# Flat PSUM quarters, a column-by-column start and an inverse term added last, in a one-core spectral and gated-MLP kernel

## The chip, the cores and the metric

The kernel runs on one core of a Trainium2 chip. The metric is the device time of one execution in microseconds. The engines are TensorE (PE for matmuls, PEld for its weight loads), VectorE (DVE), ScalarE (ACT), GpSimd (POOL) and SyncE (SP, which here only issues DMAs).

## The reference

```
xn  = layernorm(x)                      # x: 2048 x 512, bf16, over the last axis, eps 1e-5
A   = irfft2(rfft2(xn) * (w_r + i w_i)) # over both axes, w: 2048 x 257
B   = (gelu(xn @ w_gate) * (xn @ w_up)) @ w_down   # 512 -> 1792 -> 512
out = x + A + B
```

## The kernel before

The 2048 rows lie as 16 columns c of 128 rows each (row 16 p + c on partition p). Four columns form a block of 512 rows; there are four blocks. Everything is one list of operations with an engine, an expected duration, dependencies and a priority (the smaller, the earlier). A planner (`_Plan.run`) plays this list through once on the host, engine by engine, always taking the ready operation with the smallest priority, and the operations are then emitted in the order it found. So each engine's instruction order is fixed when the program is built; on the chip an engine waits at an instruction until its inputs are there.

The stages:

- **Normalization** (`layernorm`): per column, statistics on DVE (L421), their aggregate on DVE (L428), adding epsilon on POOL (L429), the power −0.5 on POOL (L431), and the scaling to `xn` on DVE (L434). Columns 0 and 1 go singly, 2 and 3 as a pair, the others in fours.
- **Transposes.** Columns 0 to 3 are transposed by PE into PSUM (L444) and copied to `xnT` by DVE (L447); columns 4 to 15 by DMA transposes from SP's queue (L451). Ahead of them PE runs nine dummy matmuls (L409), which need nothing but a memset.
- **Gate and up** (`glu`, L496): for each of 14 slices fc of 128 hidden features, four matmuls into `g_ps` and four into `u_ps`, for 128, 256 or 512 rows at once; gelu on ACT (L505), product on DVE (L510) into `hT`. In block 0 the first two fc are done for column 0, column 1 and the pair (2, 3) separately, the other twelve for all four columns.
- **Forward transform**: folds of `xn` on DVE (L538 to L550), matmuls `bp` (L564) evicted by ACT, then 16 steps `dp` (L600): four matmuls of 128 columns into one PSUM tile, each writing every second word of one half; ACT evicts the tile in order (L605). Then `ep` (L619), the filter on DVE, an exchange of partitions by DMA, and `gp` (L737), whose four matmuls write the four quarters of the tile one after the other.
- **Inverse transform and down** : `yp` (L785) per column with ACT eviction (L791) and unfolding on DVE (L807 to L813), then `down`: 14 matmuls over the hidden features (L837) and one for the inverse transform along the rows (L839), all into one PSUM tile, added to x on DVE (L842) and stored (L845). These fifteen matmuls are one operation of the plan, so it waits for `ID_[c]`, the unfolded inverse of its column.

The last column's down sum is done in two halves. PSUM tiles of the kind "S" (transposes, dummies, both transforms, down sums) share four slots, used in rotation; `g_ps` and `u_ps` have two each. Gate and up units, the spectral steps and the down sums share PE by their priorities, so the spectral chain is strewn among the gate and up matmuls. The loads at the start are issued from SP, the second x column, the identity and the first up weights from ACT. At most eight such transfers are under way at once.

Of the kernel before, what the change touches and what calls it, by code (L numbers as in the profile page):

```python
# [10 lines left out]
P = 128  # L11
BF16 = mybir.dt.bfloat16
F32 = mybir.dt.float32
I32 = mybir.dt.int32
ALU = mybir.AluOpType
# [3 lines left out]
D = 512  # L19
# [4 lines left out]
NFC = DF // P  # L24
NSB = 4
EPS = 1e-5
# [92 lines left out]

class _Buf:  # L120
    def __init__(self, tag):
        self.tag, self.left, self.users = tag, 0, 0


class _Op:
# [3 lines left out]
class _Plan:  # L129
# [17 lines left out]
        return o  # L147

    def run(self):
        free = dict(self.bufs)  # L150
        for o in self.ops:
            for b in o.use:
                b.left = b.users
        waiting = {}
        for o in self.ops:
            waiting.setdefault(o.eng, []).append(o)
        t_eng = {e: 0.0 for e in waiting}
        t_eng["PE"] = t_eng["DVE"] = t_eng["ACT"] = t_eng["POOL"] = t_eng["SP"] = 0.7
        releases, lanes, wire = [], [], 0.0
        order, left, now = [], len(self.ops), 0.0  # L160
        while left:
            releases.sort(key=lambda r: r[0])
            while releases and releases[0][0] <= now + 1e-9:
                free[releases.pop(0)[1]] += 1
            nxt, moved = None, False
            for e, ops in waiting.items():
                if not ops:
                    continue
                if t_eng[e] > now + 1e-9:
                    nxt = t_eng[e] if nxt is None else min(nxt, t_eng[e])  # L170
                    continue
                best = None
                for o in ops:
                    if any(d.end is None for d in o.deps):
                        continue
                    at = max([d.end + d.lag + self.HOP for d in o.deps if d.eng != "PE" or o.eng != "PE"] + [0.0])
                    if o.nbytes and len(lanes) >= 8:
                        at = max(at, sorted(lanes)[-8])
                    if at > now + 1e-9:
                        nxt = at if nxt is None else min(nxt, at)  # L180
                        continue
                    need = {}
                    for b in o.new:
                        need[b.tag] = need.get(b.tag, 0) + 1
                    if any(free[k] < v for k, v in need.items()):
                        continue
                    if best is None or (o.prio, o.n) < (best.prio, best.n):
                        best = o
                if best is None:
                    continue  # L190
                o, moved = best, True
                o.start = now
                o.end = now + o.dur
                t_eng[e] = o.end
                if o.nbytes:
                    wire = max(wire, o.end + 1.0) + o.nbytes / 0.3e6
                    o.end = wire + 0.8
                    lanes.append(o.end)
                    lanes = [x for x in lanes if x > now]
                for b in o.new:  # L200
                    free[b.tag] -= 1
                for b in o.use:
                    b.left -= 1
                    if not b.left:
                        releases.append((o.end + o.lag + self.HOP, b.tag))
                ops.remove(o)
                order.append(o)
                left -= 1
            if not moved:
                if releases:  # L210
                    nxt = releases[0][0] if nxt is None else min(nxt, releases[0][0])
# [9 lines left out]
def kernel(  # L221
# [43 lines left out]
    rstd = pc.tile([P, NC], F32, name="rstd")  # L265
    half = pc.tile([P, NC], F32, name="half")
    warm = pc.tile([P, D], BF16, name="warm")
    tiles = {}

    def cc(name):  # L270
# [39 lines left out]
        return dma(nbytes, fn, deps, n_dma[0] - 1000.0, eng=eng, **k)  # L310

    XD, WD = {}, {}

    def load_x(c0, n, eng="SP"):
        q = nc.sync if eng == "SP" else nc.scalar
        o = load(n * P * D * 2, lambda: q.dma_start(out=x_t[:, c0:c0 + n], in_=x_v[:, c0:c0 + n]), eng=eng)
        for c in range(c0, c0 + n):
            XD[c] = o
# [14 lines left out]
        return load(P * 2 * (b - a), lambda: q.dma_start(out=CT[:, a:b], in_=cap[:, a:b]), eng=eng)  # L333

    load_x(0, 1)
    load_x(1, 1, "ACT")
    d_ident = load_ct("ident", "ident", "ACT")
    load_w(0, 2, ("SP", "ACT"))
    load_x(2, 2)
    load_w(2, 4)  # L340
    load_x(4, 4)
    load_w(4, 7)
# [58 lines left out]
    o_mem = [add("POOL", 0.3, lambda: nc.gpsimd.memset(warm[:], 1.0), (), -20, lag=0.05),  # L401
             add("POOL", 0.2, lambda: nc.gpsimd.memset(half[:], -0.5), (), -15, lag=0.05)]
    wb = _Buf("S")
    NWARM = 9

    def warm_mm(i):
        if i == 0:
            psum("warm", [P, D])
        nc.tensor.matmul(tiles["warm"][:], lhsT=warm[:, 0:P], rhs=warm[:], start=True, stop=True)  # L409

    for i in range(NWARM):
        pe(0.43, lambda i=i: warm_mm(i), (o_mem[0],), -100 + i, new=(wb,) if i == 0 else (), use=(wb,))

# [6 lines left out]
        tiles["st", c] = st  # L420
        V.bn_stats(out=st[:], in_=x_t[:, c])  # L421

    def layernorm(c0, n, due):
        k = slice(c0, c0 + n)
        ag = []
        for c in range(c0, c0 + n):
            s = dve(0.6, lambda c=c: stats(c), (XD[c],), due - 3.0 + 0.01 * (c - c0))
            ag.append(dve(0.08, lambda c=c: V.bn_aggr(out=mv[:, c], in_=tiles["st", c][:]), (s,), due - 3.2, ))  # L428
        e = add("POOL", 0.25, lambda: nc.gpsimd.tensor_scalar(  # L429
            out=ve[:, k], in0=mv[:, k, 1], scalar1=1.0, scalar2=EPS, op0=ALU.mult, op1=ALU.add), ag, due - 5, lag=0.1)  # L430
        r = add("POOL", 0.3, lambda: nc.gpsimd.tensor_tensor(  # L431
            out=rstd[:, k], in0=ve[:, k], in1=half[:, k], op=ALU.pow), (e, o_mem[1]), due - 5, lag=0.1)
        for c in range(c0, c0 + n):
            XN[c] = dve(0.34, lambda c=c: V.tensor_scalar(  # L434
                out=xn[:, c], in0=x_t[:, c], scalar1=mv[:, c, 0:1], scalar2=rstd[:, c:c + 1],
                op0=ALU.subtract, op1=ALU.mult), (r,), due - 2.5)

    def pe_transpose(c, due):
        b = _Buf("S")

        def mm():
            tp = psum(f"tp.{c}", [P, NE, P], BF16)
            for e in range(NE):
                nc.tensor.transpose(tp[:, e], xn[:, c, e * P:(e + 1) * P], ident)  # L444

        o = pe(0.24, mm, (XN[c], d_ident), due - 2, new=(b,))
        XT[c] = dve(0.34, lambda: V.tensor_copy(out=xnT[c // 4][:, :, c % 4], in_=tiles[f"tp.{c}"][:]),  # L447
                    (o,), due - 30, use=(b,))

    def dma_transpose(c, due):  # L450
        XT[c] = dma(P * D * 2, lambda: nc.sync.dma_start_transpose(out=xnT[c // 4][:, :, c % 4], in_=xn[:, c]),  # L451
                    (XN[c],), due - 30, lag=1.0)

    for c0, n, due in ((0, 1, -20), (1, 1, -19), (2, 2, -18)):
        layernorm(c0, n, due)
        for c in range(c0, c0 + n):
            pe_transpose(c, due)
    for b, due in ((1, 16), (2, 24), (3, 32)):
        layernorm(4 * b, 4, due)
        for c in range(4 * b, 4 * b + 4):  # L460
# [55 lines left out]
            HT.setdefault(c, []).append(h)  # L516
        return h

    units = [(0, 1, 0), (0, 1, 1), (1, 1, 0), (1, 1, 1), (2, 2, 0), (2, 2, 1)]
    units += [(0, 4, fc) for fc in range(2, NFC)]  # L520
    for u in units:
        glu(*u)

# [70 lines left out]
    def dstep(G, t):  # L594
        sb, db = _Buf("S"), _Buf("ds")

        def mm():
            dp = psum(f"dp.{G}", [P, 2, P, 2])
            for q in range(4):
                nc.tensor.matmul(dp[:, q % 2, :, q // 2], lhsT=Bs[:, q, G].rearrange("p c r a -> p (c r a)"),  # L600
                                 rhs=FQ[q], start=(q == 0), stop=(q == 3), skip_group_check=True)

        def ev():
            ds = work(f"ds.{G}", [P, D], "ds")
            nc.scalar.copy(out=ds[:], in_=tiles[f"dp.{G}"][:].rearrange("p s k t -> p (s k t)"))  # L605

        p = pe(0.34, mm, [PS_[cg, q] for cg in range(4) for q in range(4)] + [d_ct], t, new=(sb,))
        DS_[G] = act(0.53, ev, (p,), t - 5, new=(db,), use=(sb,)), db

    def cstep(g, t):  # L610
# [210 lines left out]
    def down(c, t):  # L821
# [8 lines left out]
        for k in range(parts):  # L830
# [3 lines left out]
            def mm(k=k, s=s):  # L834
                y = psum(f"yp_.{c}.{k}", [P, D])
                for f in range(NFC):
                    nc.tensor.matmul(y[:, s], lhsT=tiles[sb, f][:, cl * P:(cl + 1) * P], rhs=tiles["Wd"][:, f, s],  # L837
                                     start=(f == 0), stop=False)
                nc.tensor.matmul(y[:, s], lhsT=tiles["RI"][:, c], rhs=tiles["yt"][:, c, s], start=False, stop=True)  # L839

            p = pe(15 * 0.2158 / parts, mm, HT[c] + d_wd + [d_ri, ID_[c]], t + k * 0.01, new=(pb,))
            a = dve(0.61 / parts, lambda k=k, s=s: V.tensor_tensor(  # L842
                out=tiles[f"y.{c}"][:, s], in0=tiles[f"yp_.{c}.{k}"][:, s], in1=tiles[f"y.{c}"][:, s], op=ALU.add),
                (p, l), t - 40, use=(pb, yb))
# [43 lines left out]
```

## Time and profile before

| | |
|---|---|
| median of 3 runs | 189.26 us (188.01 to 189.47) |
| the profiled execution | 188.04 us |
| its span | 186.3 us |
| mean granted clock of TensorE | 0.988 |
| busy: PE, DVE, ACT, POOL | 176.2, 119.2, 93.2, 16.7 us |

The span is the time from the first to the last recorded instruction of the profiled execution; 1.74 us lie around it. A row of the order of time gives start, duration, engine, line, operation, output and inputs, the count of instructions merged, and in brackets the idle time before it with what ended it. A row of groups gives count, total busy time, mean duration in ns, idle time before, and what ended that. PE's busy time is that of overlapping records, so a group of matmuls costs the distance to the next group's start, not its own duration. The chain of work that ended last has these distances already. In rows of DMA issues the last number is the time from issue to landing, in us.

### The profile page before, as it was taken

The numbers are of one execution on the slowest core, as the hardware profiler recorded it, in microseconds if no ns is written. First come the engines' busy times: TensorE is split into PE (matmuls) and PEld (weight loads), VectorE is DVE, ScalarE is ACT, GpSimd is POOL, SyncE is SP. The second block draws the span as 40 slices with busy tenths as digits, with TensorE's granted clock in tenths as the row PEclk, the third lists the DMA queues.
The fourth block names the chain that finished last, engine by engine and source line by source line (L and its number), as shares of the span: only waits on it lengthen the run. The fifth ranks groups of instructions, "written<-read, shape, count | busy, mean of one in ns | idle before, by whom it ended". The sixth has DMA issues, their size and how long they took to land.

```text
span 186.3 us, 2911 instructions
## 1 busy us (share of the span) xinstructions
PE 176.2 (95%) x1014; PEld 93.5 (50%) x1032; DVE 119.2 (64%) x264; ACT 93.2 (50%) x169; POOL 16.7 (9%) x35
## 2 busy tenths in 40 slices
PE   7379999999999999999999999998999999999993
PEld 2266445546545545556456545455444444444462
DVE  1779989989248999888586888247712134433521
ACT  2023348898986878798969864457200011121100
POOL 3312176230020000000000000000000000000000
PEclk9879999999999999999999999999999999999999
DMA  5999999933356010222011020200021313122111
GB/s 158 332 351 351 347 193 232 234 76 56 113 177 221 0 42 14 58 56 62 14 42 43 18 56 0 56 4 0 11 75 56 115 58 113 58 83 86 58 58 55
DMA packets 23038, 19.24 MB, mean 103 GB/s; under 512 B 8240, under 2 KB 21680, under 8 KB 23024
## 3 DMA queue, kind: packets, MB, share of 16 engines
q1 hardware_dynamic: 21888, 17.44, 35.4%
q0 software_dynamic: 320, 1.19, 2.3%
q10 hardware_dynamic: 816, 0.43, 0.8%
q8 instruction: 8, 0.13, 0.3%
q14 instruction: 6, 0.05, 0.1%
HBM read 13.28 MB, written 2.10 MB: 83 GB/s over the span
## 4 chain that ended last, share of the span: by engine, by line
PE 90%; DMA 3%; DVE 2%; ACT 2%; issue 1%; SPq 0%; DVEq 0%
PE g_ps L496 26%; PE u_ps L496 26%; PE dp L600 4%; DMA x_t<-in_A_x_dram 3%; PE bp L564 2%; PE gp L737 2%; PE ep L619 2%; PE yp__1693 L837 2%; PE yp__2023 L837 2%; PE yp__1880 L837 2%; PE yp__1849 L837 2%; PE yp__1804 L837 2%; PE yp__1784 L837 2%; PE yp__1744 L837 2%; PE yp__1725 L837 2%; PE yp__2049 L837 2%
## 5 line engine op out<-in xcount | busy, mean ns | idle before, releaser
L496 PE MATMUL g_ps<-xnT,Wg_sb 128*128 128x512 bf16 (+2 forms) x232 | 58.4, 370 | 1.7 <-DVE xnT L447 1.4
L496 PE MATMUL u_ps<-xnT,Wu_sb 128*128 128x512 bf16 (+2 forms) x235 | 58.3, 368 | 0.3
L510 DVE TENSOR_TENSOR hT<-u_ps,ge 128x512 bf16<-128x512 f32 (+2 forms) x60 | 39.0, 651 | 23.5 <-PE u_ps L496 21.7
L505 ACT ACTIVATE ge<-g_ps 128x512 bf16<-128x512 f32 (+2 forms) x60 | 34.2, 570 | 32.0 <-PE g_ps L496 29.2
L496 PEld LDWEIGHTS <-Wg_sb 128*128 128x128 bf16 x240 | 23.7, 103 | 24.4 <-DVE xnT L447 1.2
L837 PEld LDWEIGHTS <-hT 128*128 128x128 bf16 x238 | 23.0, 98 | 23.6 <-issue 0.2
L496 PEld LDWEIGHTS <-Wu_sb 128*128 128x128 bf16 x240 | 23.2, 100 | 23.2
L791 ACT CAST yf<-yp 128x512 bf16<-128x512 f32 x16 | 8.8, 588 | 39.3 <-PE yp L785 38.9
L627 ACT CAST E<-ep 64x512 bf16<-64x512 f32 x32 | 18.5, 579 | 3.9 <-PE ep L619 2.4
L421 DVE BATCH_NORM_STATS2 st<-x_t 128x6 f32<-128x512 bf16 x16 | 10.4, 668 | 5.2 <-DMA x_t<-in_A_x_dram 5.2
L605 ACT CAST ds<-dp 128x512 bf16<-128x512 f32 x16 | 8.6, 592 | 2.6 <-PE dp L600 2.6
L743 ACT CAST Gs<-gp 128x512 bf16<-128x512 f32 x16 | 8.7, 589 | 0.8 <-PE gp L737 0.8
L568 ACT CAST Bs<-bp 128x512 bf16<-128x512 f32 x16 | 8.5, 601 | 0.0
L600 PE MATMUL dp<-CT,Bs 128*128 128x128 bf16 x64 | 8.3, 309 | 0.0
L378 ACT COPY TW<-Ts 128x514 bf16<-128x514 bf16 (+1 forms) x12 | 8.0, 701 | 0.0
L600 PEld LDWEIGHTS <-Bs 128*128 128x128 bf16 x64 | 6.8, 129 | 1.6
L434 DVE TENSOR_SCALAR xn<-x_t,mv,rstd 128x512 bf16<-128x512 bf16 x16 | 5.8, 407 | 1.1 <-POOL rstd L431 1.1
L785 PE MATMUL yp<-CT,Gs 128*128 128x128 bf16 x64 | 5.7, 219 | 0.3
L785 PEld LDWEIGHTS <-Gs 128*128 128x128 bf16 x64 | 4.5, 97 | 3.0 <-issue 0.7
L660 DVE TENSOR_TENSOR m<-X,TW 128x1024 bf16<-128x1024 bf16 x8 | 5.5, 688 | 0.2
L666 DVE TENSOR_TENSOR m<-X,TW 128x1024 bf16<-128x1024 bf16 x8 | 5.5, 682 | 0.0
L737 PEld LDWEIGHTS <-F 128*128 128x128 bf16 x64 | 4.2, 98 | 1.9
(104 smaller groups left out, 169.5 us busy)
## 6 DMA issues: line engine op xcount, KB each, us to landing
y<-in_A_x_dram SPq DMA_DIRECT2D x16, 128.0 KB, 2.1
F<-F SPq DMA_DIRECT2D x32, 64.0 KB, 2.0
out_dram<-y SPq DMA_DIRECT2D x15, 128.0 KB, 1.7
Wd_sb<-in_B_w_down_dram SPq DMA_DIRECT2D x2, 896.0 KB, 7.4
x_t<-in_A_x_dram SPq DMA_DIRECT2D x3, 512.0 KB, 8.5
Wg_sb<-in_B_w_gate_dram SPq DMA_DIRECT2D x2, 384.0 KB, 7.4
Wu_sb<-in_B_w_up_dram SPq DMA_DIRECT2D x2, 384.0 KB, 7.8
Wg_sb<-in_B_w_gate_dram SPq DMA_DIRECT2D x2, 256.0 KB, 5.0
```

The costliest lines, as they stand in the source:

```text
L421: V.bn_stats(out=st[:], in_=x_t[:, c])
L496: nc.tensor.matmul(p[:, 0:w], lhsT=W[:, e, fc * P:(fc + 1) * P], rhs=rhs(e), start=(e == 0), stop=(e == NE - 1))
L505: nc.scalar.activation(out=e[:, 0:w], in_=tiles[f"g_ps.{key}"][:, 0:w], func=AF.Gelu_apprx_tanh)
L510: V.tensor_tensor(out=hslot(sb, fc)[:, o:o + w], in0=tiles[f"u_ps.{key}"][:, 0:w], in1=tiles[f"ge.{key}"][:, 0:w], op=ALU.mult)
L568: nc.scalar.copy(out=o, in_=tiles[f"bp.{cg}.{q}"][:].rearrange("p c (r g a) -> p (c r) g a", r=2, a=4))
L600: nc.tensor.matmul(dp[:, q % 2, :, q // 2], lhsT=Bs[:, q, G].rearrange("p c r a -> p (c r a)"), rhs=FQ[q], start=(q == 0), stop=(q == 3), ...
L605: nc.scalar.copy(out=ds[:], in_=tiles[f"dp.{G}"][:].rearrange("p s k t -> p (s k t)"))
L627: nc.scalar.copy(out=tiles[f"E.{g}"][64 * h:64 * h + 64, r], in_=tiles[f"ep.{g}.{h}"][64 * r:64 * r + 64])
L743: nc.scalar.copy(out=o, in_=tiles[f"gp.{g}.{h}"][:].rearrange("p q (n a) -> p (q n) a", a=4))
L785: nc.tensor.matmul(yp[:, q], lhsT=tiles["G"][:, q, c], rhs=IQ[q], start=(q == 0), stop=(q == 3), skip_group_check=True)
L791: nc.scalar.copy(out=tiles[f"yf.{c // 2}"][:, c % 2], in_=tiles[f"yp.{c}"][:])
L837: nc.tensor.matmul(y[:, s], lhsT=tiles[sb, f][:, cl * P:(cl + 1) * P], rhs=tiles["Wd"][:, f, s], start=(f == 0), stop=False)
```

## The change

- **`dp`**: the tile is declared [2, 2, 128] in place of [2, 128, 2], so that each of the four matmuls writes 128 words in a row. The eviction reads the tile by a permuted view, so `ds` is laid out as before. The expected duration in the plan goes from 0.34 to 0.222.
- **Start**: columns 0 to 3 are normalized one by one; column 1's statistics wait for column 0's aggregate. The addition of epsilon is done by DVE in all groups. The transposes of columns 0 to 3 are copied by ACT. Ten dummies in place of nine, and four more of 128 columns after each of the first two transposes. The x columns 2 and 3 are loaded singly, column 1 from SP's queue. A gelu of one element per partition, on a tile filled by POOL, stands early on ACT. Slices fc 0 to 3 of block 0 are now split: fc 0 and 1 for column 0 and for column 1, fc 2 and 3 for the pair (0, 1), and all four for the pair (2, 3).
- **`down`**: the 14 matmuls and the inverse term are two operations; only the second waits for the unfolded inverse and the row table.
- **Planner**: it follows the rotation of the slots (a tile is given a slot when the tile that held that slot is done) rather than a count of free slots.

```diff
     def run(self):
-        free = dict(self.bufs)
+        rings = {tag: [] for tag in self.bufs}
...
-                    need = {}
-                    for b in o.new:
-                        need[b.tag] = need.get(b.tag, 0) + 1
-                    if any(free[k] < v for k, v in need.items()):
+                    held = [rings[b.tag][-self.bufs[b.tag]] for b in o.new if len(rings[b.tag]) >= self.bufs[b.tag]]
+                    if any(b.free is None for b in held):
+                        continue
+                    at = max([b.free for b in held] + [0.0])
+                    if at > now + 1e-9:
+                        nxt = at if nxt is None else min(nxt, at)
                         continue
...
+    o_eps = add("POOL", 0.15, lambda: nc.gpsimd.memset(eps[:], EPS), (), -30, lag=0.05)
...
     load_x(0, 1)
-    load_x(1, 1, "ACT")
     d_ident = load_ct("ident", "ident", "ACT")
+    load_x(1, 1)
     load_w(0, 2, ("SP", "ACT"))
-    load_x(2, 2)
+    add("ACT", 1.3, lambda: nc.scalar.activation(out=eps[:, 1:2], in_=eps[:, 0:1], func=AF.Gelu_apprx_tanh),
+        (o_eps,), -900)
+    load_x(2, 1)
+    load_x(3, 1)
     load_w(2, 4)
...
-    NWARM = 9
+    NWARM, NGAP, GAP = 10, 2, 4
...
-    def layernorm(c0, n, due):
+    def layernorm(c0, n, due, after=()):
...
-            s = dve(0.6, lambda c=c: stats(c), (XD[c],), due - 3.0 + 0.01 * (c - c0))
+            s = dve(0.6, lambda c=c: stats(c), [XD[c]] + list(after), due - 3.0 + 0.01 * (c - c0))
...
-        e = add("POOL", 0.25, lambda: nc.gpsimd.tensor_scalar(
-            out=ve[:, k], in0=mv[:, k, 1], scalar1=1.0, scalar2=EPS, op0=ALU.mult, op1=ALU.add), ag, due - 5, lag=0.1)
+        e = dve(0.07, lambda: V.tensor_scalar(
+            out=ve[:, k], in0=mv[:, k, 1], scalar1=EPS, scalar2=None, op0=ALU.add), ag, due - 5)
...
-        XT[c] = dve(0.34, lambda: V.tensor_copy(out=xnT[c // 4][:, :, c % 4], in_=tiles[f"tp.{c}"][:]),
+        XT[c] = act(0.45, lambda: nc.scalar.copy(out=xnT[c // 4][:, :, c % 4], in_=tiles[f"tp.{c}"][:]),
...
-    for c0, n, due in ((0, 1, -20), (1, 1, -19), (2, 2, -18)):
-        layernorm(c0, n, due)
-        for c in range(c0, c0 + n):
-            pe_transpose(c, due)
+    first = ()
+    for c, due in ((0, -28), (1, -25), (2, -22), (3, -19)):
+        o = layernorm(c, 1, due, first if c == 1 else ())
+        first = o if c == 0 else first
+        pe_transpose(c, due)
+        if c < NGAP:
+            dummies(GAP, due - 1.9, (XN[c],), P)
...
-    units = [(0, 1, 0), (0, 1, 1), (1, 1, 0), (1, 1, 1), (2, 2, 0), (2, 2, 1)]
-    units += [(0, 4, fc) for fc in range(2, NFC)]
+    units = [(0, 1, 0), (0, 1, 1), (1, 1, 0), (1, 1, 1), (0, 2, 2), (0, 2, 3)]
+    units += [(2, 2, fc) for fc in range(4)] + [(0, 4, fc) for fc in range(4, NFC)]
...
-            dp = psum(f"dp.{G}", [P, 2, P, 2])
+            dp = psum(f"dp.{G}", [P, 2, 2, P])
             for q in range(4):
-                nc.tensor.matmul(dp[:, q % 2, :, q // 2], lhsT=Bs[:, q, G].rearrange("p c r a -> p (c r a)"),
+                nc.tensor.matmul(dp[:, q % 2, q // 2], lhsT=Bs[:, q, G].rearrange("p c r a -> p (c r a)"),
...
-            nc.scalar.copy(out=ds[:], in_=tiles[f"dp.{G}"][:].rearrange("p s k t -> p (s k t)"))
+            nc.scalar.copy(out=ds[:].rearrange("p (s k t) -> p s k t", s=2, t=2),
+                           in_=tiles[f"dp.{G}"][:].rearrange("p s t k -> p s k t"))
...
-                nc.tensor.matmul(y[:, s], lhsT=tiles["RI"][:, c], rhs=tiles["yt"][:, c, s], start=False, stop=True)
-
-            p = pe(15 * 0.2158 / parts, mm, HT[c] + d_wd + [d_ri, ID_[c]], t + k * 0.01, new=(pb,))
+            def mm2(k=k, s=s):
+                nc.tensor.matmul(tiles[f"yp_.{c}.{k}"][:, s], lhsT=tiles["RI"][:, c], rhs=tiles["yt"][:, c, s],
+                                 start=False, stop=True)
+
+            p = pe(14 * 0.2158 / parts, mm, HT[c] + d_wd, t + k * 0.01, new=(pb,))
+            p = pe(0.2158 / parts, mm2, [p, d_ri, ID_[c]], t + k * 0.01 - 2, use=(pb,))
```

More of the change, by code (lines that the diff above doesn't have):

```diff
@@ L121, in __init__ @@
     def __init__(self, tag):
-        self.tag, self.left, self.users = tag, 0, 0
+        self.tag, self.left, self.users, self.free = tag, 0, 0, None
 class _Op:
@@ L158, in run @@
         t_eng["PE"] = t_eng["DVE"] = t_eng["ACT"] = t_eng["POOL"] = t_eng["SP"] = 0.7
-        releases, lanes, wire = [], [], 0.0
+        lanes, wire = [], 0.0
         order, left, now = [], len(self.ops), 0.0
         while left:
-            releases.sort(key=lambda r: r[0])
-            while releases and releases[0][0] <= now + 1e-9:
-                free[releases.pop(0)[1]] += 1
             nxt, moved = None, False
@@ L200, in run @@
                 for b in o.new:
-                    free[b.tag] -= 1
+                    rings[b.tag].append(b)
                 for b in o.use:
@@ L204, in run @@
                     if not b.left:
-                        releases.append((o.end + o.lag + self.HOP, b.tag))
+                        b.free = o.end + o.lag + self.HOP
                 ops.remove(o)
@@ L209, in run @@
             if not moved:
-                if releases:
-                    nxt = releases[0][0] if nxt is None else min(nxt, releases[0][0])
                 if nxt is None or nxt <= now:
@@ L267 @@
     warm = pc.tile([P, D], BF16, name="warm")
+    eps = pc.tile([P, 2], F32, name="eps")
     tiles = {}
@@ L403, with warm_mm, dummies @@
     wb = _Buf("S")
-    NWARM = 9
-    def warm_mm(i):
-        if i == 0:
+    NWARM, NGAP, GAP = 10, 2, 4
+    def warm_mm(w):
+        if "warm" not in tiles:
             psum("warm", [P, D])
-        nc.tensor.matmul(tiles["warm"][:], lhsT=warm[:, 0:P], rhs=warm[:], start=True, stop=True)
-    for i in range(NWARM):
-        pe(0.43, lambda i=i: warm_mm(i), (o_mem[0],), -100 + i, new=(wb,) if i == 0 else (), use=(wb,))
+        nc.tensor.matmul(tiles["warm"][:, 0:w], lhsT=warm[:, 0:P], rhs=warm[:, 0:w], start=True, stop=True)
+    def dummies(n, prio, deps=(), w=D):
+        for i in range(n):
+            pe(w / 1200.0, lambda w=w: warm_mm(w), [o_mem[0]] + list(deps), prio + 0.01 * i,
+               new=() if wb.users else (wb,), use=(wb,))
+    dummies(NWARM, -100)
     XN, XT = {}, {}
@@ L426, in layernorm @@
         for c in range(c0, c0 + n):
-            s = dve(0.6, lambda c=c: stats(c), (XD[c],), due - 3.0 + 0.01 * (c - c0))
-            ag.append(dve(0.08, lambda c=c: V.bn_aggr(out=mv[:, c], in_=tiles["st", c][:]), (s,), due - 3.2, ))
-        e = add("POOL", 0.25, lambda: nc.gpsimd.tensor_scalar(
-            out=ve[:, k], in0=mv[:, k, 1], scalar1=1.0, scalar2=EPS, op0=ALU.mult, op1=ALU.add), ag, due - 5, lag=0.1)
-        r = add("POOL", 0.3, lambda: nc.gpsimd.tensor_tensor(
+            s = dve(0.6, lambda c=c: stats(c), [XD[c]] + list(after), due - 3.0 + 0.01 * (c - c0))
+            ag.append(dve(0.15, lambda c=c: V.bn_aggr(out=mv[:, c], in_=tiles["st", c][:]), (s,), due - 3.2, ))
+        e = dve(0.07, lambda: V.tensor_scalar(
+            out=ve[:, k], in0=mv[:, k, 1], scalar1=EPS, scalar2=None, op0=ALU.add), ag, due - 5)
+        r = add("POOL", 0.55, lambda: nc.gpsimd.tensor_tensor(
             out=rstd[:, k], in0=ve[:, k], in1=half[:, k], op=ALU.pow), (e, o_mem[1]), due - 5, lag=0.1)
         for c in range(c0, c0 + n):
-            XN[c] = dve(0.34, lambda c=c: V.tensor_scalar(
+            XN[c] = dve(0.36, lambda c=c: V.tensor_scalar(
                 out=xn[:, c], in0=x_t[:, c], scalar1=mv[:, c, 0:1], scalar2=rstd[:, c:c + 1],
                 op0=ALU.subtract, op1=ALU.mult), (r,), due - 2.5)
+        return ag
     def pe_transpose(c, due):
@@ L604, in ev @@
             ds = work(f"ds.{G}", [P, D], "ds")
-            nc.scalar.copy(out=ds[:], in_=tiles[f"dp.{G}"][:].rearrange("p s k t -> p (s k t)"))
-        p = pe(0.34, mm, [PS_[cg, q] for cg in range(4) for q in range(4)] + [d_ct], t, new=(sb,))
+            nc.scalar.copy(out=ds[:].rearrange("p (s k t) -> p s k t", s=2, t=2),
+                           in_=tiles[f"dp.{G}"][:].rearrange("p s t k -> p s k t"))
+        p = pe(0.222, mm, [PS_[cg, q] for cg in range(4) for q in range(4)] + [d_ct], t, new=(sb,))
         DS_[G] = act(0.53, ev, (p,), t - 5, new=(db,), use=(sb,)), db
```

## The prediction

> **What bounds the kernel now.** I read the page first, then the span cut into stretches, then the chain of work that ended last, and last the order of time at the two ends of the program.
>
> ```profile
> span 186.3 us, 2911 instructions
> PE 176.2 (95%) x1014; PEld 93.5 (50%) x1032; DVE 119.2 (64%) x264; ACT 93.2 (50%) x169; POOL 16.7 (9%) x35
> ```
> ```profile
> 4.00:14.00 10.00, 5.69 (x54) 4.38 (x52) 7.42 (x23) 1.11 (x4) 2.38 (x6) 0.83 1.07 341
> 14.00:45.30 31.30, 31.09 (x186) 16.39 (x189) 30.09 (x66) 20.59 (x39) 11.61 (x16) 1.00 0.98 221
> 49.40:101.34 51.94, 51.63 (x293) 28.12 (x298) 40.02 (x91) 42.61 (x76) 1.21 (x6) 1.00 0.25 72
> ```
>
> The columns of a stretch are its length and the busy time of PE, PEld, DVE, ACT and POOL, then granted clock, DMA share and GB/s. From 14 us on PE is never without work, so there only fewer or cheaper matmuls, or a PE that reaches this stretch sooner, can help. Before 14 us PE is busy 5.69 of 10 us, at a mean clock of 0.83: that is where time lies open. DVE is busy 30.09 of 31.30 us up to 45.3, ACT 42.61 of 51.94 after 49.4; both are near enough to full to be watched.
>
> The profiled execution took 188.04 us, 1.74 beside its span; the median of the runs shown is 189.26, 1.2 above. The sum is made from 188.04. About 1% (1.9 us) is what a measurement of this kernel can tell from no change.
>
> **The start.** In order of time:
>
> ```profile
> 1.31 3.64 PE L409 MATMUL warm<-warm 128*128 128x512 bf16 x9 [1.31 <-POOL half L402]
> 4.00 0.69 DVE L421 BATCH_NORM_STATS2 st<-x_t 128x6 f32<-128x512 bf16 x1 [4.00 <-DMA x_t<-in_A_x_dram]
> 5.21 0.17 DVE L428 BATCH_NORM_AGGREGATE mv<-st 128x2 f32<-128x6 f32 x1
> 6.01 0.58 POOL L431 TENSOR_TENSOR rstd<-ve,half 128x1 f32<-128x1 f32 x1
> 6.71 0.69 DVE L421 BATCH_NORM_STATS2 st<-x_t 128x6 f32<-128x512 bf16 x1 [1.21 <-DMA x_t<-in_A_x_dram]
> 7.33 0.40 DVE L434 TENSOR_SCALAR xn<-x_t,mv,rstd 128x512 bf16<-128x512 bf16 x1
> 7.78 1.01 PE L444 MATMUL tp<-CT,xn 128*128 128x128 bf16 x8 [2.83 <-DVE xn L434]
> 8.63 0.41 DVE L447 COPY xnT<-tp 128x512 bf16<-128x512 bf16 x1
> 9.09 0.59 PE L496 MATMUL g_ps<-xnT,Wg_sb 128*128 128x128 bf16 x4 [0.30 <-DVE xnT L447]
> 10.32 0.63 PE L496 MATMUL u_ps<-xnT,Wu_sb 128*128 128x128 bf16 x4
> 10.75 0.63 PE L496 MATMUL g_ps<-xnT,Wg_sb 128*128 128x128 bf16 x4
> 11.45 0.39 PE L496 MATMUL g_ps<-xnT,Wg_sb 128*128 128x128 bf16 x4
> 11.67 0.39 PE L496 MATMUL u_ps<-xnT,Wu_sb 128*128 128x128 bf16 x4
> 13.85 0.61 PE L496 MATMUL g_ps<-xnT,Wg_sb 128*128 128x256 bf16 x4 [1.05 <-DVE xnT L447]
> 14.29 0.60 PE L496 MATMUL u_ps<-xnT,Wu_sb 128*128 128x256 bf16 x4
> 19.06 1.03 PE L496 MATMUL g_ps<-xnT,Wg_sb 128*128 128x512 bf16 x4
> ```
>
> Three losses are seen. Column 0 has its statistics by 4.69, but its aggregate stands behind column 1's statistics until 5.21, and its normalization at 7.33 behind column 2's. The transpose at 7.78 is copied only at 8.63, behind DVE's next statistics. And PE was idle 2.83 us, so its clock fell: four narrow matmuls go every 0.43 us (10.32 to 10.75) until about 11.2, and every 0.22 us after (11.45 to 11.67).
>
> After the change column 1's statistics wait for column 0's aggregate, so that goes at 4.69. The addition of epsilon moves to DVE; no row shows it there. Bounds are a small gain (POOL's own addition and a hop go away) and 0.40 us, the wide normalization's row; I take 0.17, as the aggregate's row has no more elements. So 4.69 + 0.17 + 0.17 + 0.58 for the power and two hops of 0.1 between engines (an estimate; 7.73 to 7.78 is 0.05 from DVE to PE): normalization at 5.8, transposes at 6.25 (7.33 to 7.78 now), at full clock done by 6.65. The copy on ScalarE is not in the trace; its nearest rows are DVE's own copy above, 0.41, and an eviction of as many elements:
>
> ```profile
> L791 ACT CAST yf<-yp 128x512 bf16<-128x512 f32 x16 | 8.8, 588 | 39.3 <-PE yp L785 38.9 <-DVE lv L809 0.4
> ```
>
> These are the bounds, with the eviction's 0.59 taken, since it is the same engine reading PSUM; ACT is busy 1.11 us of ten here, so nothing stands behind the copy. So the first gate matmul starts at **7.3** in place of 9.09. DVE sheds four copies and takes seven small additions: nearly even.
>
> The ten dummies end near 5.2 (one more at 0.22 us, and the memset of epsilon ahead of them, some 0.1). PE then idles 1.05 us to 6.25. An idle time of just 1.05 us, at 13.85, did not slow the four matmuls behind it (0.44 us for 256 columns). So I reckon at full clock; the short dummies behind the first two transposes lie under the copies. From 7.3: eight groups of narrow matmuls at 0.22 (1.76), twelve of 256 columns at 0.44 (5.28), two transposes and the last dummies (0.66): fc 4 starts at **15.0** in place of 19.06. The early table load and the wait for epsilon stand in ACT's idle time, with no copy due before 6.65; behind that wait on ACT is nothing but compute.
>
> Column 1 moves from ACT's queue to SP's, ahead of the first gate weights; the split of columns 2 and 3 adds one issue.
>
> ```profile
> 1.65 0.52 ACTq L326 DMA_DIRECT2D Wu_sb<-in_B_w_up_dram  x1
> 2.19 0.43 SPq L326 DMA_DIRECT2D Wg_sb<-in_B_w_gate_dram  x1
> ```
> ```profile
> Wu_sb<-in_B_w_up_dram ACTq DMA_DIRECT2D x1, 256.0 KB, 6.0
> Wg_sb<-in_B_w_gate_dram SPq DMA_DIRECT2D x1, 256.0 KB, 6.1
> SPq L316 <- DMA x_t<-in_A_x_dram: 1.0, 1, 1.0
> ```
>
> The first up weights land at 7.65 now; issued 0.45 us sooner with 128 KB less ahead on their queue they land at 6.5 to 7.2, in time for 7.5. The second gate weights land at 8.3. Their up half becomes the ninth transfer, the one that waits for the first to land (4.0 us); at the 341 GB/s of this stretch its 256 KB come 0.75 us behind, at about 9.1, and PE wants them at 9.7. That is tight by half a microsecond.
>
> **Where the start's gain is cut.** Block 1 needs the DMA transposes of columns 4 to 7:
>
> ```profile
> 24.43 2.60 SPq L451 DMA_TRANSPOSE xnT<-xn  x1
> ```
> ```profile
> xnT<-xn SPq DMA_TRANSPOSE x1, 9.2
> SPq L451 <- DMA Wu_sb<-in_B_w_up_dram: 0.9, 1, 0.9
> ```
> ```profile
> 36.52 0.89 PE bp L564 x16
> 38.27 0.86 PE g_ps L496 x4
> ```
>
> The first of the four was held by the landing of a weight transfer (second row of waits), the fourth, issued at 24.43, landed at 33.63. The same bytes stand ahead of them after the change, so I leave 33.63. PE would come to block 1 at 15.0 + 10 units of 1.73 (twice 0.86) + one transform group of 0.89 = 33.2; it must wait to 33.7. Now it comes there at 38.27 less 0.17 (a group's record of 1.03 at 19.06 against the chain's 0.86: records overlap), 38.1, with one transform group (0.89) more done: 37.2. **Gain 3.5**, not 4.1. The wait absorbs half a microsecond of error in the start.
>
> **The forward transform.**
>
> ```profile
> 63.39 0.87 PE dp L600 x8
> 73.77 0.45 PE gp L737 x8
> ```
> ```profile
> L605 ACT CAST ds<-dp 128x512 bf16<-128x512 f32 x16 | 8.6, 592 | 2.6 <-PE dp L600 2.6
> L600 PEld LDWEIGHTS <-Bs 128*128 128x128 bf16 x64 | 6.8, 129 | 1.6
> ```
>
> Eight dp matmuls take 0.87 us and eight gp of the same shape 0.45; gp writes its quarters flat, dp every second word. Flat, each of the eight pairs saves 0.42: **3.4**. The eviction now reads words from two quarters by turns. No row reads PSUM so; its bounds are 0.59 (nothing changes) and 1.18 (each word dear twice, as for dp). I take 0.59: ScalarE wants one word where PE writes two in the same time (512 columns in 0.216 us against 0.588 for the row). ACT's 42.61 us of work then stand in some 49 us, and small waits of PE on it are likely: I charge **0.5**. DVE finishes the folds only some 2 us sooner, as it is full to 45.3; gate and up matmuls of blocks 1 to 3 cover that, and it would cost 1.5 us without them.
>
> **The end of the gate and up work.**
>
> ```profile
> 126.66 2.93 PE L785 MATMUL yp<-CT,Gs 128*128 128x128 bf16 x32
> 127.08 2.56 ACT L791 CAST yf<-yp 128x512 bf16<-128x512 f32 x5 [0.49 <-PE yp L785]
> 128.49 0.42 DVE L811 TENSOR_TENSOR yt<-lv 128x512 bf16<-128x512 bf16 x1
> 129.69 3.18 PE L837 MATMUL yp__1693<-Wd_sb,hT 128*128 128x512 bf16 x13
> ```
>
> Eight inverse steps take 3.03 us here, paced by ScalarE's evictions, and would take 0.22 each by the gp row, which has the same form: 1.25 us lost. The first down sums no longer wait for their inverse term, so they stand between the steps: **1.2**. The number of matmuls is unchanged, as is the tail behind the last one.
>
> Sum: 188.04 − 3.5 − 3.4 − 1.2 + 0.5 = **180.4 us**, chance 0.68.
>
> **Rivals.**
> - *The DMA transposes come later.* If the added transfer shifts the landing that the first one waits for by one place, to the x columns behind the weights (512 KB at 341 GB/s are 1.5 us), block 1 starts 1.5 later: 181.9. For it: transfers wait on each other eight back. Against: the transposes move one place too. 0.08.
> - *The clock is not held.* If it falls in the 1.05 us, or is granted late, the narrow work runs at half speed for some 1.5 us more; fc 4 comes at 16.5, block 1 at 34.7: 181.4. 0.06. [...]
> - *The eviction costs double.* 16 more times 0.43 us (half of the 0.86 that 512 words at half rate would take) makes ACT's work 6.9 longer: 49 us in 49, so PE waits some 3: 183.4. 0.06.
> - *The change does not do what it says at dp:* its weight loads (129 against 98 ns) set the pace, not the writes. Nothing of the 3.4: 183.8. Against: a load's 129 ns is already more than the spacing of 109 ns (0.87 by 8), so loads overlap and need not set it. 0.05. [...]
> - *Slower: down sums hold the PSUM ring.* A down sum now keeps one of four S slots until its inverse term is there. If three stand ahead of the next inverse pair, that pair waits, and its chain of eviction and unfolding (126.66 to 128.9, 2.25 us) lies open. Over eight pairs that is 18 us: 199. From five pairs on it is slower than now. Against: inverse steps are ordered more than two columns ahead. 0.04.
>
> **How the numbers follow.** The low end: no wait for the transposes (4.1 for the start), the copy and the epsilon at their low ends (0.35), no charge on ACT, the full 1.25 at the end: 178.9, and 0.4 for what executions differ, 178.5. The high end: the fourth rival's 183.8 and the 1.2 us between profile and median, 185.0. What lies outside is the last rival and 0.03 for several losses together that bring it within 1%; all else is faster by over 1%: 0.93, 0.03, 0.04.
>
> **What the changed profile would show.** First gate matmul near 7.3, clock at 1.0 from about 5 us on, fc 4 near 15; PE waiting for DMA at the start of block 1, near 33.7; eight dp in 0.45 us with ds rows still near 590 ns; down sums standing among the first inverse steps, with no waits of PE behind ScalarE there. The prediction is wrong if ds rows are over 0.8 us, if weights land after 7.5 or 9.7, or if PE has gaps over 1 us after 34 us.

## The result, and the profile after

The changed kernel takes **181.22 us** (median of 4 runs, 180.84 to 181.63) against 189.25 before (4 runs, one more than shown above): a ratio of 0.9589, 95% interval 0.9542 to 0.9635. Forecast were 180.4 us in a range of 178.5 to 185.0. The profiled execution took 181.31 us, 1.81 beside its span.

The page, and two stretches of the span (length, then PE, PEld, DVE, ACT and POOL busy, clock, DMA share, GB/s):

```profile
span 179.5 us, 2986 instructions
PE 173.6 (97%) x1057; PEld 91.0 (51%) x1057; DVE 117.9 (66%) x269; ACT 95.6 (53%) x176; POOL 16.4 (9%) x31
```
```profile
4.00:14.00 10.00, 9.33 (x95) 7.22 (x94) 8.80 (x30) 4.68 (x12) 2.21 (x4) 1.00 1.05 341
14.00:45.30 31.30, 30.68 (x185) 15.91 (x184) 28.53 (x66) 20.46 (x39) 11.48 (x13) 1.00 0.88 213
```

Up to 14 us PE is now busy 9.33 of 10 us at a granted clock of 1.00 (5.69 at 0.83 before). From 14 to 45.3 us it is busy a little less than before (30.68 against 31.09): new waits are there. The start in order of time:

```profile
1.34 4.45 PE L411 MATMUL warm<-warm 128*128 128x512 bf16 x10 [1.34 <-POOL half L404]
3.65 0.69 DVE L427 BATCH_NORM_STATS2 st<-x_t 128x6 f32<-128x512 bf16 x1 [3.65 <-DMA x_t<-in_A_x_dram]
5.52 0.41 DVE L440 TENSOR_SCALAR xn<-x_t,mv,rstd 128x512 bf16<-128x512 bf16 x1
5.99 0.61 PE L451 MATMUL tp<-CT,xn 128*128 128x128 bf16 x4 [0.20 <-DVE ve L435]
6.39 0.63 PE L411 MATMUL warm<-warm 128*128 128x128 bf16 x4
6.63 0.58 ACT L454 COPY xnT<-tp 128x512 bf16<-128x512 bf16 x1 [3.45 <-PE tp L451]
7.27 0.38 PE L506 MATMUL g_ps<-xnT,Wg_sb 128*128 128x128 bf16 x4 [0.25 <-ACT xnT L454]
8.38 0.39 PE L506 MATMUL u_ps<-xnT,Wu_sb 128*128 128x128 bf16 x4
9.00 0.38 PE L506 MATMUL g_ps<-xnT,Wg_sb 128*128 128x128 bf16 x4 [0.23 <-ACT xnT L454]
15.57 1.89 PE L506 MATMUL g_ps<-xnT,Wg_sb 128*128 128x512 bf16 x8
32.01 1.03 PE L506 MATMUL g_ps<-xnT,Wg_sb 128*128 128x512 bf16 x4
33.31 1.02 PE L506 MATMUL u_ps<-xnT,Wu_sb 128*128 128x512 bf16 x4 [0.27 <-DVE hT L520]
34.17 1.03 PE L506 MATMUL g_ps<-xnT,Wg_sb 128*128 128x512 bf16 x4
35.77 0.84 PE L574 MATMUL bp<-RF_t,xf 128*128 128x128 bf16 x12 [0.35 <-DVE xf L560]
69.48 1.02 PE L506 MATMUL u_ps<-xnT,Wu_sb 128*128 128x512 bf16 x4 [0.37 <-DVE hT L520]
```

The first gate matmul stands at 7.27, fc 4 at 15.57, block 1 at 34.17. The four transposes at 5.99 take 0.40 us and the ten dummies 4.45, about 0.43 each for 512 columns: that is half the pace of the groups from 7.27 on (0.22), although the granted clock is 1.00 in the row above. The spectral steps and the first down sums, from the chain of work that ended last and from the groups:

```profile
74.39 0.45 PE dp L610 x8
121.41 0.45 PE yp L796 x8
121.86 3.02 PE yp__1688 L848 x14
```
```profile
L615 ACT CAST ds<-dp 128x512 bf16<-128x512 f32 x16 | 9.0, 590 | 1.1 <-PE dp L610 1.0
L610 PEld LDWEIGHTS <-Bs 128*128 128x128 bf16 x64 | 4.3, 98 | 1.9
```

Eight dp matmuls take 0.45 us, their eviction by turns from two quarters 590 ns (592 before), and a down sum begins right behind the third inverse step. Three places remain where PE waits after 16 us (33.31, 35.77 and 69.48). The first is between 32.01 and 33.31: 1.30 us for a group of 0.86. Its cause lies on ScalarE:

```profile
29.02 0.62 ACT L380 COPY TW<-Ts 128x514 bf16<-128x514 bf16 x1 [3.15 <-DMA Ts<-in_A_w_r_dram]
16.66 1.09 POOL L365 DMA_INDIRECT Ts<-in_A_w_r_dram,idx_t  x1 [0.18 <-issue]
30.17 0.69 DVE L520 TENSOR_TENSOR hT<-u_ps,ge 128x512 bf16<-128x512 f32 x1 [2.24 <-ACT ge L515]
```
```profile
Ts<-in_A_w_r_dram SPq DMA_DIRECT2D x2, 224.9 KB, 13.2
```

ScalarE waited 3.15 us for filter rows loaded from SP, with a gelu behind the wait in its queue; a product on DVE waited 2.24 us for that gelu. The chain of work that ended last goes through this load, and from it by the gelu and DVE to PE at 35.77:

```profile
15.80 13.14 DMA Ts<-in_A_w_r_dram
```

Before the change the same two loads landed 10.4 us after issue (these lines give KB of one and the median from issue to landing), the gathers of the other filter rows on GpSimd began at 24.14 us and no copy waited:

```profile
Ts<-in_A_w_r_dram SPq DMA_DIRECT2D x2, 224.9 KB, 10.4
```
```profile
24.14 1.10 POOL L363 DMA_INDIRECT Ts<-in_A_w_r_dram,idx_t  x1 [0.17 <-issue]
27.52 0.62 ACT L378 COPY TW<-Ts 128x514 bf16<-128x514 bf16 x1
```

The gathers moved because the plan gave GpSimd another order. Before, the addition and the power of columns 8 to 11 (at 22.34 and 22.96) stood ahead of them; now that power (23.60) stands behind them.

### The profile page after: what moved, and what is told of

Read it like the earlier page. It is cut to its first block, busy times and chain, and to the rows that moved or that the text cites. A ratio compares the mean times of both kernels' runs of the same rounds, so it can differ in the third digit from the quotient of the medians.

```text
span 179.5 us, 2986 instructions
## 1 busy us (share of the span) xinstructions
PE 173.6 (97%) x1057; PEld 91.0 (51%) x1057; DVE 117.9 (66%) x269; ACT 95.6 (53%) x176; POOL 16.4 (9%) x31
## 4 chain that ended last, share of the span: by engine, by line
PE 73%; DMA 9%; DVE 7%; SPq 6%; issue 2%; ACT 1%; ACTq 0%; DVEq 0%
PE u_ps L506 18%; PE g_ps L506 17%; DMA Ts<-in_A_w_r_dram 7%; SPq L325 3%; DMA Wu_sb<-in_B_w_up_dram 2%; PE yp L796 2%; PE gp L748 2%; SPq L315 2%; DVE hT L520 2%; PE yp__2064 L848 2%; PE yp__2037 L848 2%; PE yp__2006 L848 2%; PE yp__1921 L848 2%; PE yp__1890 L848 2%; PE yp__1863 L848 2%; PE yp__1832 L848 2%
## 5 line engine op out<-in xcount | busy, mean ns | idle before, releaser
L515 ACT ACTIVATE ge<-g_ps 128x512 bf16<-128x512 f32 (+2 forms) x62 | 35.0, 564 | 21.9 <-PE g_ps L506 15.6
L506 PEld LDWEIGHTS <-Wg_sb 128*128 128x128 bf16 x248 | 23.2, 98 | 22.0 <-issue 0.8
L802 ACT CAST yf<-yp 128x512 bf16<-128x512 f32 x16 | 9.3, 586 | 38.1 <-PE yp L796 38.1
L437 POOL TENSOR_TENSOR rstd<-ve,half 128x1 f32<-128x1 f32 (+1 forms) x7 | 6.7, 955 | 24.8 <-DVE ve L435 24.8
L411 PE MATMUL warm<-warm 128*128 128x512 bf16 (+1 forms) x18 | 5.5, 469 | 1.3 <-POOL half L404 1.3
L630 PE MATMUL ep<-ds,CT 128*128 128x512 bf16 x16 | 5.6, 379 | 0.0
```

Source lines behind the costliest of these rows:

```text
L506: nc.tensor.matmul(p[:, 0:w], lhsT=W[:, e, fc * P:(fc + 1) * P], rhs=rhs(e), start=(e == 0), stop=(e == NE - 1))
L515: nc.scalar.activation(out=e[:, 0:w], in_=tiles[f"g_ps.{key}"][:, 0:w], func=AF.Gelu_apprx_tanh)
L802: nc.scalar.copy(out=tiles[f"yf.{c // 2}"][:, c % 2], in_=tiles[f"yp.{c}"][:])
```

## Experiments: the parts one by one

The kernel before, measured again beside each of three groups of runs, had medians of 188.95, 188.89 and 189.56 us, so a difference between kernels of different groups is good to about half a microsecond.

**The flat tile alone**, put into the kernel before:

```diff
-            dp = psum(f"dp.{G}", [P, 2, P, 2])
+            dp = psum(f"dp.{G}", [P, 2, 2, P])
...
-        p = pe(0.34, mm, ...
+        p = pe(0.222, mm, ...
```

> The kernel before with the flat dp tile, its permuted eviction and its shorter planned duration alone. Theory (the writes of every second word set dp's pace): eight dp matmuls in 0.45 us, eviction rows near 590 ns, 3.4 us less than before, ratio near 0.982. Rival (another engine paces the chain there, or the work goes into a new wait): less than 1.5 us.

185.54 us (185.25 to 185.64) against 188.95, ratio 0.9814 (0.9786 to 0.9841): 3.4 us. In its chain and groups:

```profile
63.16 0.45 PE dp L600 x8
```
```profile
L605 ACT CAST ds<-dp 128x512 bf16<-128x512 f32 x16 | 8.7, 592 | 1.8 <-PE dp L600 1.7
```

The term stands at its full size, and nothing of it went into a wait.

**The old tile in the changed kernel** (the same edit backwards):

> The changed kernel with the old dp tile, eviction and planned duration. Theory (terms add up): 3.4 us more than the changed kernel, about 184.6. Rival (the order of the plan or the fuller ScalarE ate part of the gain): 2 us more or less than that, 182 to 183.2.

184.00 us (183.56 to 185.39), 2.8 more than the changed kernel's 181.22; eight dp take 0.87 us again. This lies between the two expectations. The runs of this kernel differ by 1.8 us, so the missing 0.6 is not settled.

**The old start in the changed kernel**: normalization, copies, loads, dummies and units of `before`, with flat dp, split down sums and the new planner.

> The changed kernel with everything of the start as before (normalization of 2 and 3 as a pair, copies on DVE, epsilon on POOL, nine dummies, old loads and units); flat dp, split down sums and new planner stay. Theory (block 1 starts 3.1 us sooner with the new start, and some 1 us of that goes into waits of PE on DVE behind it): 2 to 3.1 us more than the changed kernel, 183.2 to 184.3. Rival (the start is absorbed by the load stream later): under 1 us more.

183.95 us (182.93 to 184.99): 2.7 more, as the theory had it. In its profiled execution narrow matmuls went at half pace for longer than in that of the kernel before:

```profile
9.64 0.58 PE L493 MATMUL g_ps<-xnT,Wg_sb 128*128 128x128 bf16 x4 [0.28 <-DVE xnT L444]
12.58 0.63 PE L493 MATMUL u_ps<-xnT,Wu_sb 128*128 128x128 bf16 x4
13.01 1.06 PE L441 MATMUL tp<-CT,xn 128*128 128x128 bf16 x8
```

Eight narrow groups run from 9.64 to 13.01 at some 0.42 us each, where before five did (9.09 to 11.18). If the old start's time depends on when the full clock is granted, that would account for the spread of its runs, 2.1 us against 0.8 for the changed kernel; only one of these runs has a trace, so this is not shown.

**Joined down sums in the changed kernel:**

```diff
-            p = pe(14 * 0.2158 / parts, mm, HT[c] + d_wd, t + k * 0.01, new=(pb,))
-            p = pe(0.2158 / parts, mm2, [p, d_ri, ID_[c]], t + k * 0.01 - 2, use=(pb,))
+            p = pe(15 * 0.2158 / parts, mm, HT[c] + d_wd + [d_ri, ID_[c]], t + k * 0.01, new=(pb,))
```

> The changed kernel with the 14 down matmuls and the inverse term as one operation again; the orders differ only from the first inverse steps on. Theory (the steps ahead of the first down sum are paced by ScalarE's evictions): 1.2 us more, about 182.4, with eight inverse steps in some 3 us. Rival (no cost, since gate and up work could cover the steps): within 0.4 us.

182.79 us (181.81 to 183.40), 1.6 more. In order of time:

```profile
122.09 2.94 PE L796 MATMUL yp<-CT,Gs 128*128 128x128 bf16 x32
125.13 3.18 PE L848 MATMUL yp__1734<-Wd_sb,hT 128*128 128x512 bf16 x13
```

Eight inverse steps in 3.04 us again, 1.26 more than at 0.22 each; the other 0.3 lies within what the runs differ.

Taken out of the changed kernel one at a time, the tile, the start and the split down sums are worth 2.8, 2.7 and 1.6 us, 7.1 of the 8.0 between the two medians.

**The old planner in the changed kernel** (`run` and its count of free slots as before):

> The changed kernel with the old planner, which counts free slots in place of following their rotation; all other edits stay. Theory (PE had next to no waits of that kind before either, so the planner's model is worth little): within 0.5 us of the changed kernel. Rival (with down sums holding PSUM slots until their inverse term, an order that ignores the rotation makes inverse steps wait): 2 us or more slower, with PE's waits at the inverse steps.

180.80 us (180.60 to 181.09), beside 181.09 (180.78 to 181.39) for the changed kernel measured beside it, whose run had been announced so:

> The changed kernel itself, beside the other kernels of this job: 181.2 us again, within 0.4.

The ranges overlap. Following the rotation brings nothing here that can be measured, and the order without it holds no waits at the inverse steps.

## Experiments: the clock, and what the start's gain runs into

**Two dummies only**, the order being the same:

```diff
     def warm_mm(w):
+        n_warm[0] += 1
+        if n_warm[0] > 2:
+            return
```

> The changed kernel with two wide dummies only, in the same order otherwise (the other eight wide ones and the eight short ones are left out, which changes no result). PE is then idle from about 2.2 to 6.0 us. Theory (the dummies buy the full clock for the narrow work): four narrow matmuls every 0.43 us for some 3.4 us from the first transpose on, fc 4 1.2 to 1.6 us later, and 0.8 to 1.5 us more in all. Rival (ScalarE's wait for the row tables and DVE behind it set the pace anyway before block 1): fc 4 later, but under 0.4 us more in all.

182.09 us (181.99 to 182.45): 0.9 more. In order of time:

```profile
6.11 0.61 PE L456 MATMUL tp<-CT,xn 128*128 128x128 bf16 x4 [3.73 <-DVE ve L440]
8.19 0.63 PE L511 MATMUL g_ps<-xnT,Wg_sb 128*128 128x128 bf16 x4
8.62 0.63 PE L456 MATMUL tp<-CT,xn 128*128 128x128 bf16 x4
17.23 1.03 PE L511 MATMUL g_ps<-xnT,Wg_sb 128*128 128x512 bf16 x3
```

After 3.73 us without work the narrow groups go every 0.43 us up to 11.15, some 5 us from the first transpose on (6.11); 3.4 were expected, which is what the kernel before showed (7.78 to 11.18). fc 4 starts at 17.23, 1.66 later. Of this 0.9 reaches the end; the rest takes the place of waits that the sooner start runs into: this kernel has none between 32 and 36 us. So the dummies, wide and short together, buy about a third of the start's 2.7 us. How short an idle time costs the clock is open: behind 2.83 us (before) the granted clock was 0.50 from 7.85 to 11.26 us, behind 1.05 us 256 columns went in 0.44 us at 1.00.

**Later copies on ScalarE**: only the plan is told that the SP loads of filter rows come 4 us later, so that the copies stand further back in ScalarE's order.

```diff
-                d_st[k, s] = [load(64 * R7 * 2, lambda k=k, s=s, h=h: load_rows(k, s, h)) for h in range(2)]
+                d_st[k, s] = [load(64 * R7 * 2, lambda k=k, s=s, h=h: load_rows(k, s, h), lag=4.0) for h in range(2)]
```

> The changed kernel with 4 us added in the plan alone to the time at which the four SyncE loads of filter rows are taken to be there, so that ScalarE's copies of them stand later in its order; the transfers themselves are not touched. Theory (the harm is ScalarE's place in the queue, not the transfer): ScalarE's wait on that transfer falls under 0.5 us, PE's waits between 32 and 36 us vanish, 0.5 to 1.0 us less in all. Rival (DVE is full there): no change within 0.3 us.

**180.16 us** (179.95 to 180.31), 1.1 less than the changed kernel. The first copies of rows loaded from SP now start at 33.62:

```profile
33.62 1.17 ACT L380 COPY TW<-Ts 128x514 bf16<-128x514 bf16 x2
```

In the waits of this kernel's PE no engine is waited for after the start; these are all:

```profile
PE warm L411 <- POOL half L404: 1.3, 1, 1.3
PE tp L451 <- DVE xn L440: 0.5, 1, 0.5
PE g_ps L506 <- ACT xnT L454: 0.5, 2, 0.2
```

The changed kernel has two more, on DVE, and one at the transform:

```profile
PE u_ps L506 <- DVE hT L520: 0.6, 2, 0.4
PE bp L574 <- DVE xf L560: 0.4, 1, 0.4
```

One execution of each does not show the cause: fc 4 starts 0.48 us later here (16.05) than in the changed kernel's, and the profile of the old planner, whose plan is the changed kernel's up to some 60 us, has no wait on DVE either, with fc 4 at 16.19. Two other runs settle it. The kernel with joined down sums has the changed kernel's order at this place, the one with the repair below has the late copies. Both start fc 4 alike (16.23 and 16.24), and both get the rows late, 14.2 and 14.0 us after issue. The first waits, the second does not wait anywhere after the start:

```profile
34.15 1.02 PE L506 MATMUL u_ps<-xnT,Wu_sb 128*128 128x512 bf16 x4 [0.36 <-DVE hT L520]
```
```profile
Ts<-in_A_w_r_dram SPq DMA_DIRECT2D x2, 224.9 KB, 14.0
```

So the waits between 32 and 36 us came from ScalarE's place in line, not from DVE being full.

**Later gathers on GpSimd**: in the plan, the two wide gathers wait for the constants.

```diff
-                d_st[k, s] = [add("POOL", 1.2, ..., (g_idx, XD[12]), 20, lag=5.0)]
+                d_st[k, s] = [add("POOL", 1.2, ..., (g_idx, XD[12], d_ct), 20, lag=5.0)]
```

> The changed kernel with the two wide GpSimd gathers of filter rows held back until the constants have landed, so that they start near 24 us, as before the change, and not at 16.7. Theory (they take the DMA engines from the SyncE loads of the other filter rows, whose late landing blocks ScalarE, then DVE, then PE): the first row load lands near 26 in place of 29 us, ScalarE's wait of 3.2 us shrinks under 1, PE's waits between 32 and 36 us fall from about 1.0 to under 0.3, and 0.5 to 1.0 us less in all. Rival (DVE is simply full there): the waits between 32 and 36 us stay, no change within 0.3 us.

180.64 us (180.37 to 180.75), 0.6 less. ScalarE and PE in order of time:

```profile
27.28 0.62 ACT L380 COPY TW<-Ts 128x514 bf16<-128x514 bf16 x1 [1.40 <-DMA Ts<-in_A_w_r_dram]
```
```profile
32.02 1.03 PE L506 MATMUL g_ps<-xnT,Wg_sb 128*128 128x512 bf16 x4
32.88 1.03 PE L506 MATMUL u_ps<-xnT,Wu_sb 128*128 128x512 bf16 x4
33.75 1.03 PE L506 MATMUL g_ps<-xnT,Wg_sb 128*128 128x512 bf16 x4
```

The rows land 1.7 us sooner (27.28 against 29.02), the wait falls from 3.15 to 1.40, and PE reaches block 1 at 33.75 with no wait, from the same fc 4 (15.59). The wide gathers start at 26.52, later than announced, and two gathers of a seventh of their width take their place at 16.54 and 17.94. Their early start thus delays the loads here, though by less than expected (29 to 26). Most other profiles agree: with wide gathers from 16.7 to 17.2 us the two loads land 13.2 to 14.6 us after issue (four profiles), with gathers from 24.14 us or later after 9.6 to 11.8 (five). The kernel with two dummies does not fit: GpSimd's order is the changed kernel's there, and the loads landed after 11.5 us. This run and the one before remove the waits between 32 and 36 us from two sides; the wait near 69 us stays here (0.38 us of idle time).

**The repair of the first filter row in seven operations**, on top of the later copies. The changed kernel's third wait, at 69 us, stood behind seven small DVE instructions planned as one.

```diff
-            last = dve(2.2, s10, [last], t, new=(ab,), use=(eb, fb))
+            for i in range(7):
+                last = dve(0.42 if i < 6 else 0.1, lambda i=i: s10(i), [last], t, new=(ab,) if i == 0 else (),
+                           use=(ab, eb, fb))
```

> The changed kernel with ScalarE's copies of the filter rows later in the plan (as in the run that gained 1.1 us), and the repair of the first filter row, seven small DVE instructions in a row, as seven operations of the plan in place of one. Theory (the seven, 2.4 us in one piece, kept a product waiting and PE behind it for 0.5 us near 69 us): that wait goes, 0.3 to 0.6 us less than with the later copies alone, about 179.7. Rival (the products come in time there or DVE is late elsewhere): no change against 180.16 within 0.2.

180.25 us (179.92 to 180.67). A miss: with the later copies the products already came in time there, so there was nothing left to gain. With the late gathers as well:

> As the run before, with the two wide GpSimd gathers also held back until the constants have landed. Theory (both edits remove the same wait of ScalarE, so they do not add up): within 0.3 us of the run before. Rival (late gathers also bring the DMA transposes of block 1 sooner, and PE waits for these): 0.4 us less or more.

180.19 us (180.05 to 181.00): the two do not add up. The later copies alone are as good as any kernel that was run.

**Pairs of words**, to see what the strided writes pay for:

```diff
-            dp = psum(f"dp.{G}", [P, 2, 2, P])
+            dp = psum(f"dp.{G}", [P, 2, 64, 2, 2])
...
-                nc.tensor.matmul(dp[:, q % 2, q // 2], ...
+                nc.tensor.matmul(dp[:, q % 2, :, q // 2, :], ...
```

> The changed kernel with dp writing pairs of neighbouring words, the pairs four words apart, and an eviction that reads accordingly. [...] Rival (any gap in the output slows the writes): eight in 0.87 us, 2.8 us more in all, as with every second word.

181.12 us (180.69 to 181.60), the changed kernel's time; in the chain and the groups:

```profile
74.43 0.45 PE dp L610 x8
```
```profile
L610 PEld LDWEIGHTS <-Bs 128*128 128x128 bf16 x64 | 4.3, 98 | 1.9
```

Eight matmuls take the 0.45 us of the flat tile and not the rival's 0.87: output in pairs with gaps costs nothing here, every second word costs double. The weight loads are the same in all three forms, but take 98 ns in both fast ones and 129 with single words, so they follow the writes' pace and do not set it.

## Why the prediction was right, point by point

- **Start to the first gate matmul:** 7.3 forecast, 7.27 measured, and two deviations cancel in it. Column 0 of x landed at 3.65 in place of 4.00, so the normalization (5.52) and the transposes (5.99) came some 0.3 sooner than forecast. The transposes went at half pace, so the copy began 0.64 us behind their start (6.63) and not 0.40. The copy took 0.58 us (0.59 taken). That the sum fits to 0.03 is luck; in a second profile of the changed kernel, with transposes at full pace (four in 0.24 us), the gate matmul stands at 6.98.
- **From there to fc 4:** 15.0 forecast, 15.57 measured. The sum had two transposes behind the first gate matmul where there are three (0.22), and no wait for the second column's copy (0.40: 8.38 to 9.00 less a group of 0.22). PE was at full pace in this stretch (0.22 us a group), but not as reckoned: the full pace did not come near 5 us. The slow dummies (0.43 each) lasted to 5.79, so PE was idle 0.20 us and not 1.05, and the full pace came between 6.39 and 7.27, just ahead of the gate matmuls. Whether the short dummies, which the prediction gave no value of their own, had a part in that was not run.
- **Block 1:** 33.7 forecast, 34.17 measured, a gain of 3.05 against the 3.5 taken. Here the reason was wrong. The step held that the DMA transposes would be waited for, because "the same bytes stand ahead of them". More bytes did: the wide gathers had moved ahead of the row loads. Yet the last transpose that block 1 needs landed before it was wanted:

```profile
27.62 2.26 SPq L458 DMA_TRANSPOSE xnT<-xn  x1
```
```profile
xnT<-xn SPq DMA_TRANSPOSE x1, 5.7
```

27.62 + 5.7 is 33.3, ahead of 34.17, and of the 33.73 at which PE would have come without its wait of 0.44 (1.30 less 0.86). What PE waited for was a product, held by a gelu, held by a copy, held by the row loads, which landed 13.2 us after issue in place of 10.4. The prediction named gate and up weights, x columns and transposes among the transfers that a sooner start could run into; it did not follow the filter rows, whose copies share ScalarE's queue with the gelus.
- **Flat dp:** 3.4 forecast, 3.4 measured alone. The eviction's price of 0.59 us held (590 ns).
- **Inverse steps:** 1.2 forecast, 1.26 by the trace, 1.6 by the times, whose runs differ by more than that gap.
- **Charge for ACT and DVE:** 0.5 was taken behind block 1; the trace has 0.52 at the second transform group (35.03 to 35.77 less 0.22) and 0.54 near 69 us (68.08 to 69.48 less 0.86). This term was too small by about half a microsecond. The first part comes from ScalarE's wait at 29 us, which could have been charged as one; the second stands behind seven small DVE instructions (65.81 to 68.42).
- **Sum:** from block 1 to PE's end 146.03 us before (37.22 to 183.25, where 37.22 is 38.11 less the transform group of 0.89 that stands ahead there) and 142.43 after (34.17 to 176.60): 3.6 gained, where 3.4 + 1.2 − 0.5 = 4.1 were forecast. Half a microsecond short there and 0.45 at the start make the 0.9 us by which the profiled execution (181.31) lies above 180.4.
- **What was luck:** the forecast gain was 7.6 us. The profiled executions differ by 6.7 (188.04 to 181.31), the medians by 8.0 (189.25 to 181.22). The prediction took its base from an execution 1.2 us below the median and set the result beside a median; the shortfall of 0.9 and this difference partly cancel. From the median the same terms would have given 181.6, 0.4 too much.
- **Rivals:** the clock rival's loss did not occur, though its condition was half met: the full pace came late (after 6.39 us), but before the gate matmuls (7.27), and the idle time that might have cost the clock was not there (0.20 us). The run with two dummies gives its price, 0.9 us (1.0 reckoned). The dear eviction is refuted (590 ns); the 0.43 us that it took for 512 words at full rate fits the gelu rows of the kernel before (277 ns for 128 words, 599 for 512: 0.84 ns for each further word). So are the weight loads as the pace (98 ns once the tile was flat, 129 before). Late transposes did not decide. The down sums held no inverse step: with the split, steps and sums alternate, and under either planner PE has no wait there. In that rival's own sums, 180.4 + 18 is 198.4 and not 199, and four pairs (9.0 us) would already have lost to 188.04, not five.

## What to carry to other kernels

When a stage is moved sooner, list for every engine in order what it waits for that does not move, the load stream above all: here ScalarE, in order, reached a transfer early, waited 3.15 us and blocked the work behind it, and PE, two engines away, showed the wait (0.44 us). Giving the planner a later landing time for one transfer was worth 1.1 us, more than a planner that models slots better. For matmul output, lay PSUM tiles so that neighbouring words go together, and let the eviction do the permuting: here eight matmuls took 0.45 us and not 0.87, and the eviction 590 ns beside 592.

## What the runs showed of the hardware

- For TensorE's output, two neighbouring words cost as much with gaps between the pairs as without (eight matmuls of 128 columns in 0.45 us), single words with gaps 0.87 us.
- ScalarE read PSUM by turns from two places 512 bytes apart at no cost: 590 ns for 512 words, 592 in order.
